# One step in sixteen rounded instead of f32 with its low part on GpSimd, a later transposition, and a new tail, in a fused attention and expert kernel

## The chip, the cores and the metric

The kernel runs on one core of a Trainium2 chip. Its time is the device time of one execution in microseconds (us). The core's engines work side by side, each through its own queue in program order: TensorE (PE in the profile, its weight loads PEld), VectorE (DVE), ScalarE (ACT), GpSimd (POOL) and SyncE (SP), which here only issues transfers. An instruction that waits holds up all that stands behind it in its queue.

## The reference

```python
B, N, C, n_agents = 4, 12480, 128, 49
a2k     = softmax(scale * agents @ k.T)      # 49 x 12480 for each batch
agent_v = a2k @ v                            # 49 x 128
q2a     = softmax(scale * q @ agents.T)      # 12480 x 49
x       = q2a @ agent_v                      # 12480 x 128, for 4 batches
h = x @ w_in                                 # d_ff = 2048
g = h - np.tanh(h)
out = g @ w_out
```

All is f32. The kernel multiplies `agent_v` by `w_in` once for each batch (the tile pair `awh`, `awl`), so that `h` comes straight from `q2a`.

## The kernel before

**Blocks, steps and pairs.** The tokens of the four batches are cut into 100 blocks of 500 (the last of each batch has 480). The 2048 hidden units are cut into 8 chunks of 256. One step is one block with one chunk, 800 steps in all. Here a **block pair** is two neighbouring blocks, thus 16 steps, and a step's place in it is its **position** 0 to 15 (`pos`). There are 50 block pairs, numbered 0 to 49.

**One step.** PE makes `h` (line 563, two halves of 128 x 504, six short products); ACT takes tanh (`y`, line 573) and squares it (`z`, line 578); DVE multiplies `h` by `z`, which gives `g` (line 583). For the small `h` of these inputs `h * z` is close enough to `h - tanh(h)`. Then PE multiplies `g` by a chunk of `w_out` and adds it to the block's accumulator `acc` (line 632), in one of two ways:

- a **rounded** step splits `g`: GpSimd rounds it to `gh` (line 613), DVE takes `gl = g - gh` (line 618), and PE multiplies `gh` and `gl` by split weights, 12 short products;
- a **plain** step multiplies `g` by unsplit f32 weights: nothing on GpSimd, no second DVE instruction, 4 products that the trace records as 8.

`PLAIN` holds the positions that are plain: 1, 3, 7, 8 and 9. So GpSimd rounds eleven times in a block pair.

**The order around the change.** It is written out by hand in `fast`. In the turn of step k the program emits: the take-over of a finished block (ACT copies half of `acc`, line 644; DVE adds the other half to it, line 641, after which the accumulator's bank is free), then `product(k)`, that is `g` and for a rounded step `gh`; then the running side jobs, one stage each; then tanh and square of step k+1; then `h` of a step ahead; then `gl` of step k-1; then the products of step k-1 into `acc`. `AHEADS` says which `h` a turn makes: two steps ahead as a rule, but at position 8 both of positions 10 and 11, at position 9 none. A finished block is taken over two turns after its last products, so that the even block of the pair is taken over at position 10 and the odd one at position 2.

**Side jobs.** One job makes the softmax over agents for the queries of the next block pair. It begins at position 2; its stages are spread by `QGAPS`, and its last stage falls on position 9: DVE sums (line 521), adds a small constant (522), inverts (523), scales `qe` (524) and copies it rounded into `pp` (527), and GpSimd writes the rest into `pp` (529). `pp` is then transposed on PE in two halves (line 538), at positions `T0` = 11 and `T1` = 15; one turn later ACT casts the result into `pT` (547) and two transfers copy it to other partitions (`pb`, lines 551 and 552). `h` of the next block pair reads `pT` and `pb`; its first one is made at position 14. While a batch is worked on, key jobs (`KS`) and value jobs (`VS`) prepare the next batch; a value job subtracts the maximum on GpSimd (line 344). `kq` is the list of jobs still to come.

**Buffers.** PSUM has four places of two banks, shared by `h`, `acc`, `pt` and the jobs. SBUF tiles: `g` four, `gh` three, `gl` three.

**The end.** After the last step, the last products are made, the last block is taken over, and one transfer (line 809) stores both blocks of the last pair.

Of the kernel before, what the change touches and what calls it, by code (L numbers as in the profile page):

```python
# [12 lines left out]
F32 = mybir.dt.float32  # L13
# [6 lines left out]
ALU = mybir.AluOpType  # L20
# [38 lines left out]
KV = 3  # L59
VB = 4  # L60
PLAIN = (1, 3, 7, 8, 9)
NB = dict(y=2, z=2, g=4, gh=3, gl=3)
Q0 = 2
NV = 10
# [3 lines left out]
QL = 0  # L68
QS = 2
QGAPS = (1, 1, 0, 2, 3, 0, 0)  # L70
T0 = 11
T1 = 15
KS = {2: 1, 12: 2}
VS = {1: 1, 8: 2}
# [4 lines left out]
def width(n):  # L79
    return min(BLK, N - n % NBLK * BLK)  # L80


def column(n):
    return n // NBLK * N + n % NBLK * BLK
# [18 lines left out]
class Build:  # L103
# [31 lines left out]
    def constants(self):  # L135
# [17 lines left out]
        self.wo_l = c.tile([128, NCH, C], F32R, tag="wo_l", name="wo_l")  # L153
        self.wo_f = {i: c.tile([128, 2 * C], F32, tag=f"wo_f{i}", name=f"wo_f{i}") for i in sorted({i % 8 for i in PLAIN})}
        self.vb = [c.tile([128, GT, C + 2], F32, tag=f"v{i}", name=f"v{i}") for i in range(VB)]
# [47 lines left out]
    def load_w_out(self, c, raw):  # L203
        one, two = self.wtile("gl", NB["gl"]), self.wtile("gh", NB["gh"])
        cut = lambda t, k: t[:, 512 * k : 512 * (k + 1)]
        return self.decode(raw, self.wf[:, c * 512 : (c + 1) * 512], cut(one, 0), cut(one, 1), cut(two, 0), cut(two, 1))
# [364 lines left out]
    def tanh(self, h, w):  # L571
        y = self.wtile("y", NB["y"])[:, : 2 * w]
        self.nc.scalar.activation(self.pair(y), h, AF.Tanh, scale=TSC)  # L573
        return y

    def square(self, y):
        z = self.wtile("z", NB["z"])[:, : y.shape[1]]
        self.nc.scalar.activation(z, y, AF.Square, scale=GSC)  # L578
        return z

    def mul(self, h, z, w):
        g = self.wtile("g", NB["g"])[:, : 2 * w]
        self.nc.vector.tensor_tensor(self.pair(g), h, self.pair(z), ALU.mult)  # L583
        self.mul_at = self.last_name()
        return g

    def act_general(self, hv, w):
        nc = self.nc
        d = self.wtile("y", NB["y"])[:, : 2 * w]
        u = self.wtile("z", NB["z"])[:, : 2 * w]  # L590
        nc.scalar.activation(self.pair(d), hv, AF.Tanh)
# [21 lines left out]
        self.nc.gpsimd.tensor_scalar(gh, g, 1.0, 0.0, ALU.mult, ALU.add)  # L613
        return gh

    def low(self, g, gh):
        gl = self.wtile("gl", NB["gl"])[:, : g.shape[1]].bitcast(F32R)
        self.nc.vector.tensor_tensor(gl, g, gh.bitcast(F32), ALU.subtract)  # L618
        return gl

    def m2(self, acc, i, gh, gl, wf=None):
        nc = self.nc
        w = gh.shape[1] // 2
        high, low = (lambda c: self.wo_h[:, 2 * i + c, :]), (lambda c: self.wo_l[:, 2 * i + c, :])
        if gl is None:
            terms = [(lambda c: wf[:, c * C : (c + 1) * C], gh, c) for c in range(2)]
        else:
            terms = [(low, gh, 0), (high, gh, 0), (low, gh, 1), (high, gh, 1), (high, gl, 0), (high, gl, 1)]
        for k, (weights, g, c) in enumerate(terms):
            for r in range(2):  # L630
                rows = slice(HALF * r, HALF * (r + 1))
                nc.tensor.matmul(  # L632
                    acc[:, r, :w],
                    weights(c)[rows],
                    g[rows, c * w : (c + 1) * w],
                    start=i == 0 and k == 0,
                    stop=i == NCH // 2 - 1 and k == len(terms) - 1,
                )
# [46 lines left out]
    def fast(self):  # L685
        nc, tc = self.nc, self.tc
        HP = NCH // 2
        blocks = [(b, j) for b in range(B) for j in range(NBLK)]
        steps = [(n, i) for n in range(len(blocks)) for i in range(HP)]
# [13 lines left out]
        def t_job(n):  # L703
            pT[n] = []
            return self.q_transpose(pp[n // 2][0], n % 2, pT[n])
# [84 lines left out]
        kq = []  # L790
        r1, r2, done = [], [], []
# [7 lines left out]
        def out_at(n):  # L799
            first = n - n % 2  # L800
            if n == first and n // 2 not in outs:
                outs[n // 2] = self.work.tile([128, GW], F32, tag="out", name="o", bufs=2)
            return outs[n // 2][:, n % 2 * width(first) :][:, : width(n)]

        def finish(n):
            self.add_up(out_at(n), acc[n])
            if n % 2 == 1:
                w = width(n - 1) + width(n)
                nc.sync.dma_start(self.outT[:, column(n - 1) : column(n - 1) + w], outs[n // 2][:, :w])

# [13 lines left out]
        def product(k):  # L824
            n, i = steps[k]
            g = self.mul(hs.pop(k), zs.pop(k), width(n))
            plain = n == 0 or n % 2 * HP + i in PLAIN
            gh = None if plain else self.high(g)
            r1.append((n, i, g, gh))

        def low(keep):
            while len(r1) > keep:
                n, i, g, gh = r1.pop(0)
                r2.append((n, i, g, None) if gh is None else (n, i, gh, self.low(g, gh)))

        def out(k):
            while r2:
# [12 lines left out]
        for k, (n, i) in enumerate(steps):  # L850
            b = blocks[n][0]
            pos = (n % 2) * HP + i
            p = n // 2
            if n % NBLK == 0 and i == 0 and b + 1 < B:
                kq = self.phase1(b + 1)
            begin = kq[0][0].get(pos, 0) if kq and n else 0
            if done and done[0][1] < k - 1:
                self.take(out_at(done[0][0]), acc[done[0][0]])
                finish(done.pop(0)[0])
            product(k)  # L860
            if n == LATE and i < NP:
                self.bound(0, i, slice(PCUT[i], PCUT[i + 1]))
            part = rest0.pop(0) if n == 0 and i in (0, 2, 4) else None
            go(part, 3)
            if n == 0 and i == 5:
                live.append(q1)
            if p + 1 < npair and pos in (T0, T1):
                live.append(t_job(2 * p + 2 + (pos == T1)))
# [12 lines left out]
            for j in AHEADS.get(pos, (AHEAD,)) if n else (AHEAD,):  # L881
                first_product(k + j)
            low(1)
            mark = self.last_on(ET.DVE)
            if n == 0:
# [16 lines left out]
            for kind in [x[0] for x in kq[:begin]]:  # L902
                if kind is kq[0][0] and kind.get(pos):
                    start(kq.pop(0)[1](pos))
        low(0)
        out(len(steps))
        while done:
            self.take(out_at(done[0][0]), acc[done[0][0]])
            finish(done.pop(0)[0])
# [64 lines left out]
```

## Time and profile before

| | |
|---|---|
| time, median of 3 runs | 2017.02 us (2016.4 to 2018.77) |
| the profiled execution's own time | 2018.59 us |
| its span, first to last instruction | 2016.8 us |
| mean granted clock of TensorE | 0.995 |
| PE busy, share of the span | 99% |
| DVE, ACT busy | 91%, 90% |
| GpSimd busy | 50% |
| chain that ended last: PE | 84% of the span |
| line 583, DVE `g`, 800 instructions | 955.5 us busy, 1195 ns each |
| line 618, DVE `gl`, 545 | 656.8 us busy, 1205 ns each |
| line 613, GpSimd `gh`, 545 | 853.0 us busy, 1565 ns each |

How to read it: a timeline row gives the start in us, the duration, engine, line, operation and tiles, and in brackets how long the engine sat idle before and what ended it. A row of the chain gives start, length and the work that the end waited for. A row of the windows gives a stretch, its length and the busy time of each engine in it, with the number of instructions, then the granted clock, the share of the DMA engines and GB/s. A row of the waits gives who waited for whom, the total, the number of times and the longest.

### The profile page before, as it was taken

How to read it: one execution, taken by the hardware profiler on the slowest of the kernel's cores; microseconds unless marked ns; L12 is line 12 of the kernel's file. 1: busy time of each engine (PE TensorE's matmuls, PEld its weight loads, DVE VectorE, ACT ScalarE, POOL GpSimd, SP SyncE). 2: the span in 40 equal slices, each digit the busy share in tenths (PEclk: the TensorE clock that was granted, in tenths of full speed). 3: DMA queues.
4: the chain of work that ended last, by engine and by line, in shares of the span. 5: the costliest groups of instructions: out<-in, count | busy, mean ns of one | idle time of the engine just before them, and what ended most of it. 6: DMA issues, size and time to landing. Idle time of an engine off the chain costs nothing.

```text
span 2016.8 us, 49577 instructions
## 1 busy us (share of the span) xinstructions
PE 1986.9 (99%) x20779; PEld 1460.9 (72%) x20779; DVE 1825.6 (91%) x1986; ACT 1806.5 (90%) x2052; POOL 999.9 (50%) x702
## 2 busy tenths in 40 slices
PE   8899999999999999999999999999999999999998
PEld 7477767777677777777677777777767777777775
DVE  7799999889999998898999999889899999999997
ACT  3789989899999998899999999998999999999996
POOL 1254455555445455554454454555545546555554
PEclk9899999999999999999999999999999999999999
DMA  9422112221111222221012111221101101101100
GB/s 331 135 85 93 54 45 84 83 61 44 54 61 65 78 71 60 78 75 60 31 36 92 61 58 44 71 61 56 54 29 34 52 31 35 52 29 37 39 24 27
DMA packets 76601, 129.70 MB, mean 64 GB/s; under 512 B 5384, under 2 KB 55376, under 8 KB 76368
## 3 DMA queue, kind: packets, MB, share of 16 engines
q1 hardware_dynamic: 76368, 126.44, 19.2%
q8 instruction: 165, 2.70, 0.6%
q14 instruction: 68, 0.56, 0.1%
HBM read 81.10 MB, written 25.56 MB: 53 GB/s over the span
## 4 chain that ended last, share of the span: by engine, by line
PE 84%; ACT 8%; DVE 4%; issue 2%; DMA 1%; SPq 0%; POOL 0%; DVEq 0%; POOLq 0%
PE acc L632 49%; PE h L563 26%; ACT z L578 4%; ACT y L573 4%; DVE g L583 2%; PE misc L508 2%; PE misc L357 2%; PE pt L538 1%; PE misc L301 1%; PE h L273 1%; DVE gl L618 1%; PE misc L472 1%; DMA v<-w_out 1%; PE h L380 0%; ACT s L349 0%
## 5 line engine op out<-in xcount | busy, mean ns | idle before, releaser
L613 POOL TENSOR_SCALAR gh<-g 128x1000 fp32r<-128x1000 f32 (+1 forms) x545 | 853.0, 1565 | 622.5 <-DVE g L583 578.6
L583 DVE TENSOR_TENSOR g<-h,z 128x1000 f32<-128x1000 f32 (+1 forms) x800 | 955.5, 1195 | 133.5 <-ACT z L578 122.9
L573 ACT ACTIVATE y<-h 128x1000 f32<-128x1000 f32 (+1 forms) x800 | 802.4, 1003 | 68.6 <-PE h L563 60.5
L578 ACT ACTIVATE z<-y 128x1000 f32<-128x1000 f32 (+1 forms) x800 | 831.4, 1039 | 25.4
L618 DVE TENSOR_TENSOR gl<-g,gh 128x1000 fp32r<-128x1000 f32 (+1 forms) x545 | 656.8, 1205 | 1.3 <-POOL gh L613 1.0
L563 PE MATMUL h<-pT,awh 49*128 49x504 f32 x1600 | 552.0, 424 | 0.0
L632 PE MATMUL acc<-g,wo_f 64*128 64x500 f32 (+1 forms) x1960 | 443.3, 578 | 0.0
L632 PE MATMUL acc<-gh,wo_l 64*128 64x500 f32 (+1 forms) x2180 | 433.0, 387 | 0.5 <-POOL gh L613 0.2
L632 PE MATMUL acc<-gh,wo_h 64*128 64x500 f32 (+1 forms) x2180 | 432.6, 386 | 0.0
L563 PE MATMUL h<-pT,awl 49*128 49x504 f32 x800 | 369.5, 462 | 7.2 <-DVE awl L476 3.4
L632 PE MATMUL acc<-gl,wo_h 64*128 64x500 f32 (+1 forms) x2180 | 341.2, 387 | 1.0 <-DVE gl L618 0.5
L563 PE MATMUL h<-pb,awh 49*128 49x504 f32 x1600 | 317.1, 387 | 0.0
L563 PE MATMUL h<-pb,awl 49*128 49x504 f32 x800 | 309.0, 386 | 0.0
L632 PEld LDWEIGHTS acc<-g,wo_f 64*128 64x128 f32 x1960 | 190.6, 186 | 145.3 <-issue 126.1
L563 PEld LDWEIGHTS h<-pT,awh 49*128 49x128 f32 x1600 | 265.9, 186 | 20.9 <-issue 11.1
L632 PEld LDWEIGHTS acc<-gh,wo_h 64*128 64x128 f32 x2180 | 214.3, 186 | 37.2
L632 PEld LDWEIGHTS acc<-gl,wo_h 64*128 64x128 f32 x2180 | 211.5, 184 | 40.0 <-DVE gl L618 5.7
L632 PEld LDWEIGHTS acc<-gh,wo_l 64*128 64x128 f32 x2180 | 211.1, 184 | 38.6 <-POOL gh L613 1.7
L563 PEld LDWEIGHTS h<-pT,awl 49*128 49x128 f32 x800 | 147.6, 184 | 117.4 <-DVE o L641 49.9
L529 POOL TENSOR_TENSOR pp<-qe,pp 128x392 fp32r<-128x392 f32 x50 | 51.5, 1030 | 265.3 <-DVE pp L527 257.2
L563 PEld LDWEIGHTS h<-pb,awh 49*128 49x128 f32 x1600 | 153.9, 184 | 29.9 <-DMA pb<-pT 0.5
L563 PEld LDWEIGHTS h<-pb,awl 49*128 49x128 f32 x800 | 149.3, 187 | 11.7 <-issue 6.4
(113 smaller groups left out, 1130.4 us busy)
## 6 DMA issues: line engine op xcount, KB each, us to landing
kt<-kT SPq DMA_DIRECT2D x48, 512.0 KB
qt<-qT SPq DMA_DIRECT2D x46, 500.0 KB
outT<-o SPq DMA_DIRECT2D x46, 500.0 KB
pb<-pT SPq DMA_DIRECT2D x200, 96.5 KB
v<-v SPq DMA_DIRECT2D x36, 512.0 KB
vt<-v SPq DMA_DIRECT2D x12, 512.0 KB
raw<-w_in SPq DMA_DIRECT2D x4, 512.0 KB
v<-w_out SPq DMA_DIRECT2D x4, 512.0 KB
```

What stands on the lines that cost most here:

```text
L273: nc.tensor.matmul(ps[:, t // 4, (t % 4) * A2 : (t % 4 + 1) * A2], kt[:, t, :], self.ag[:, 0:2, :], start=True, stop=True,)
L301: nc.tensor.matmul(to, kt[:, t, r : r + QUART], self.ag[:, b, :], start=True, stop=True)
L357: nc.tensor.matmul(ps[HALF * odd : HALF * odd + w, : C + 1], flat[:r, t * A : t * A + w], vt[:r, t, : C + 1], start=t < 2, stop=t >= n - 2,)
L508: nc.tensor.matmul(to, qt[:, token : token + QUART], self.ag[:, b, :], start=True, stop=True)
L529: nc.gpsimd.tensor_tensor(pp[:, :, HALF:PW], ev, pp[:, :, :A].bitcast(F32), ALU.subtract)
L563: nc.tensor.matmul(h[:, c, : BT * TT], aw[a][rows[c], sl], pT[p][rows[c], :], start=k == 0, stop=k == 2)
L573: self.nc.scalar.activation(self.pair(y), h, AF.Tanh, scale=TSC)
L578: self.nc.scalar.activation(z, y, AF.Square, scale=GSC)
L583: self.nc.vector.tensor_tensor(self.pair(g), h, self.pair(z), ALU.mult)
L613: self.nc.gpsimd.tensor_scalar(gh, g, 1.0, 0.0, ALU.mult, ALU.add)
L618: self.nc.vector.tensor_tensor(gl, g, gh.bitcast(F32), ALU.subtract)
L632: nc.tensor.matmul(acc[:, r, :w], weights(c)[rows], g[rows, c * w : (c + 1) * w], start=i == 0 and k == 0, stop=i == NCH // 2 - 1 and k == ...
```

## The change

Four things are changed.

1. Position 9 becomes a rounded step, except in the first block pair and where the next job to come is a value job. Its `gl` is made by GpSimd, right behind `gh`, in the turn of step 9 itself (`low(g, gh, True)` in `product`); the list `r1` carries it to the turn in which PE uses it. In the compiled program 37 steps are changed so; in the 12 block pairs with value jobs to come position 9 stays plain.
2. `T0` goes from 11 to 12: the first transposition, its cast and its two transfers come one turn later, in all 49 block pairs that have them.
3. The last step of the program (position 15 of the last pair) becomes plain.
4. The last two blocks are stored by a transfer each.

```diff
+POOL_LOW = (9,)
...
-T0 = 11
+T0 = 12
...
-    def low(self, g, gh):
+    def low(self, g, gh, pool=False):
         gl = self.wtile("gl", NB["gl"])[:, : g.shape[1]].bitcast(F32R)
-        self.nc.vector.tensor_tensor(gl, g, gh.bitcast(F32), ALU.subtract)
+        (self.nc.gpsimd if pool else self.nc.vector).tensor_tensor(gl, g, gh.bitcast(F32), ALU.subtract)
         return gl
...
             self.add_up(out_at(n), acc[n])
-            if n % 2 == 1:
+            if n >= len(blocks) - 2:
+                nc.sync.dma_start(self.outT[:, column(n) : column(n) + width(n)], out_at(n))
+            elif n % 2 == 1:
...
             g = self.mul(hs.pop(k), zs.pop(k), width(n))
-            plain = n == 0 or n % 2 * HP + i in PLAIN
+            pos = n % 2 * HP + i
+            pool = n > 1 and pos in POOL_LOW and not (kq and kq[0][0] is VS) and k < len(steps) - 1
+            plain = n == 0 or pos in PLAIN and not pool or k == len(steps) - 1
             gh = None if plain else self.high(g)
-            r1.append((n, i, g, gh))
+            r1.append((n, i, g, gh, self.low(g, gh, True) if pool else None))
 
         def low(keep):
             while len(r1) > keep:
-                n, i, g, gh = r1.pop(0)
-                r2.append((n, i, g, None) if gh is None else (n, i, gh, self.low(g, gh)))
+                n, i, g, gh, gl = r1.pop(0)
+                r2.append((n, i, g, None) if gh is None else (n, i, gh, gl or self.low(g, gh)))
```

What this does to the queues, at two places. From line 62 on, the changed file's numbers are higher by one, up to `finish`.

GpSimd, one block pair without value jobs, before: the rounding of positions 10 to 15, 0, 2 and 4 (nine `gh`), the query job's subtraction, the rounding of positions 5 and 6, and the rest of `pp`.

```order
L613 TENSOR_SCALAR gh<-g 128x1000 x9
L517 TENSOR_TENSOR qe<-qe,qm 128x392
L613 TENSOR_SCALAR gh<-g 128x1000 x2
L529 TENSOR_TENSOR pp<-qe,pp 128x8x49
L613 TENSOR_SCALAR gh<-g 128x1000 x9
```

And now:

```order
L614 TENSOR_SCALAR gh<-g 128x1000 x9
L518 TENSOR_TENSOR qe<-qe,qm 128x392
L614 TENSOR_SCALAR gh<-g 128x1000 x3
L619 TENSOR_TENSOR gl<-g,gh 128x1000
L530 TENSOR_TENSOR pp<-qe,pp 128x8x49
L614 TENSOR_SCALAR gh<-g 128x1000 x9
```

A third `gh` (position 9) and its `gl` now stand ahead of `pp`, and so ahead of the `gh` of position 10.

DVE at the same place, before: `g` of positions 8 and 9, the last stage of the query job, the addition that frees the accumulator, and `g` of positions 10 and 11.

```order
L583 TENSOR_TENSOR g<-h,z 128x1000 x2
L521 TENSOR_REDUCE qs<-qe 128x8
L522 TENSOR_SCALAR qs<-qs 128x8
L523 RECIPROCAL qs<-qs 128x8
L524 TENSOR_TENSOR qe<-qe,qs 128x392
L527 CAST pp<-qe 128x8x49
L641 TENSOR_TENSOR o<-o,acc 128x500
L583 TENSOR_TENSOR g<-h,z 128x1000 x2
L618 TENSOR_TENSOR gl<-g,gh 128x1000
```

In the changed program DVE's rows at this place are the same nine, in the same order, with their new line numbers; in the whole program DVE loses one `gl`, that of the last step.

PE, from the `h` of position 12 on, before: that `h`, the plain products of position 9, the transposition, and `h` of position 13.

```order
L563 MATMUL h<-pT,awl 128x504
L563 MATMUL h<-pT,awh 128x504 x2
L563 MATMUL h<-pb,awl 128x504
L563 MATMUL h<-pb,awh 128x504 x2
L632 MATMUL acc<-g,wo_f_87 128x500 x4
L538 MATMUL pt<-identr,pp 113x64 x8
L563 MATMUL h<-pT,awl 128x504
L563 MATMUL h<-pT,awh 128x504 x2
```

And now, from the products of position 9 on, with those of position 10 behind `h` of position 13:

```order
L633 MATMUL acc<-gl,wo_h 128x500 x4
L564 MATMUL h<-pT,awl 128x504
L564 MATMUL h<-pT,awh 128x504 x2
L564 MATMUL h<-pb,awl 128x504
L564 MATMUL h<-pb,awh 128x504 x2
L633 MATMUL acc<-gh,wo_l 128x500 x2
L633 MATMUL acc<-gh,wo_h 128x500 x2
L633 MATMUL acc<-gh,wo_l 128x500 x2
L633 MATMUL acc<-gh,wo_h 128x500 x2
L633 MATMUL acc<-gl,wo_h 128x500 x4
L539 MATMUL pt<-identr,pp 113x64 x8
L564 MATMUL h<-pT,awl 128x504
```

The transposition has moved behind `h` of position 13 and the products of position 10; the first row is the end of position 9's products, which now read `gl`.

## The prediction, made before the changed kernel ran

> **What bounds the kernel now.** I read the windows first, for one block pair of the last batch, where no key or value jobs run (the columns: stretch, length, busy time of PE, PEld, DVE, ACT, POOL, then the granted clock).
>
> ```profile
> 1896.61:1933.48 36.87, 36.87 (x350) 27.08 (x350) 33.98 (x37) 34.96 (x38) 19.64 (x14) 1.00 0.07 26
> ```
>
> PE is busy in all of the 36.87 us; DVE has 2.9 us to spare, ACT 1.9, GpSimd half. So PE sets the time, work taken from PE is worth its length, and any wait put on PE costs its length, unless another engine is then late. Next the chain through positions 8 to 12 of block pair 48:
>
> ```profile
> 1954.63 3.36 PE acc L632 x16
> 1957.99 0.78 PE h L563 x6
> 1958.77 1.68 PE acc L632 x8
> 1960.44 0.33 PE pt L538 x8
> 1960.77 0.76 PE h L563 x5
> 1961.53 1.36 PE acc L632 x11
> ```
>
> The 3.36 are the plain products of positions 7 and 8; then come `h` of position 12, the plain products of position 9 (1.68), the transposition, `h` of position 13 and the rounded products of position 10 (1.36). A plain step thus costs PE 0.32 us more than a rounded one: this is what the change takes away. Now what the other engines do there, from the timeline:
>
> ```profile
> 1954.07 1.20 DVE L583 TENSOR_TENSOR g<-h,z 128x1000 f32<-128x1000 f32 x1 [0.68 <-ACT z L578]
> 1955.18 0.55 DVE L521 TENSOR_REDUCE qs<-qe 128x8 f32<-128x392 f32 x1
> 1955.77 0.17 DVE L522 TENSOR_SCALAR qs<-qs 128x8 f32<-128x8 f32 x1
> ...
> 1956.21 0.57 DVE L524 TENSOR_TENSOR qe<-qe,qs 128x392 f32<-128x392 f32 x1
> 1956.81 0.36 DVE L527 CAST pp<-qe 128x392 fp32r<-128x392 f32 x1
> 1957.09 0.67 DVE L641 TENSOR_TENSOR o<-o,acc 128x500 f32<-128x500 f32 x1
> 1957.67 2.48 DVE L583 TENSOR_TENSOR g<-h,z 128x1000 f32<-128x1000 f32 x2
> 1960.11 1.20 DVE L618 TENSOR_TENSOR gl<-g,gh 128x1000 fp32r<-128x1000 f32 x1
> 1961.45 1.20 DVE L583 TENSOR_TENSOR g<-h,z 128x1000 f32<-128x1000 f32 x1
> ```
> ```profile
> 1957.26 1.03 POOL L529 TENSOR_TENSOR pp<-qe,pp 128x392 fp32r<-128x392 f32 x1 [6.30 <-DVE pp L527]
> 1959.05 1.02 POOL L613 TENSOR_SCALAR gh<-g 128x1000 fp32r<-128x1000 f32 x1 [0.77 <-DVE g L583]
> 1960.34 1.87 POOL L613 TENSOR_SCALAR gh<-g 128x1000 fp32r<-128x1000 f32 x1 [0.26 <-DVE g L583]
> ```
> ```profile
> 1957.81 0.49 PE L563 MATMUL h<-pT,awl 49*128 49x504 f32 x1
> 1962.73 0.46 PE L563 MATMUL h<-pT,awl 49*128 49x504 f32 x1
> ```
> ```profile
> PEld h L563 <- DVE o L641: 49.9, 99, 1.6
> PEld h L563 <- DVE g L583: 31.3, 106, 1.0
> ```
>
> The first row is `g` of position 9; it ends at 1955.27, and DVE goes straight into the query job. `h` of position 12 starts on PE at 1957.81, 0.05 after the addition L641 has freed the accumulator's bank (1957.09 + 0.67 = 1957.76). The waits name this pair of instructions 99 times. So **the DVE queue from L521 to L641 has no room: what delays it stops PE**. `h` of position 14 (1962.73) likewise follows `g` of position 12 (1961.45 + 1.20 = 1962.65), the second row of the waits. GpSimd's 6.30 us of idle time ahead of `pp` are where the new `gh` and `gl` go. They lie on DVE's query job.
>
> **Do GpSimd and DVE get in each other's way?** Two stretches of the timeline say so.
>
> ```profile
> 754.45 1.03 POOL L613 TENSOR_SCALAR gh<-g 128x1000 fp32r<-128x1000 f32 x1 [0.37 <-DVE g L583]
> ```
> ```profile
> 754.51 1.00 DVE L323 TENSOR_SCALAR dg<-ident,mc 49x49 f32<-49x49 f32 x1
> ```
> ```profile
> 1365.41 1.03 POOL L613 TENSOR_SCALAR gh<-g 128x1000 fp32r<-128x1000 f32 x1 [0.41 <-DVE g L583]
> ```
> ```profile
> 1365.67 1.82 DVE L618 TENSOR_TENSOR gl<-g,gh 128x1000 fp32r<-128x1000 f32 x1
> ```
>
> A small DVE instruction (49 x 49) that begins 0.06 behind a `gh` ends with it, 1.00 us later; a `gl`, 1.20 as a rule, takes 1.82 when a `gh` has begun before it. L522 is of the first kind (one SBUF tile in, one out), as L527 is, and L524 of the second (two tiles in). The other way round, the `gh` of 1960.34, begun behind the `gl` of 1960.11, takes 1.87 instead of 1.02. So the two exclude each other, the later one waits for the end of the earlier, where DVE reads SBUF alone. `g` and L641 read PSUM too and run beside `gh` undisturbed (1959.05, inside 1957.67 + 2.48).
>
> **The new schedule in block pair 48.** `gl` of 1000 on GpSimd is in no row. Its nearest kin:
>
> ```profile
> L214 POOL TENSOR_TENSOR wo_l<-awh,wo_h x4: 1274/1294/1487, 78.7 to 90.1; 128x512 fp32r<-128x512 f32 x4
> ```
> ```profile
> L344 POOL TENSOR_TENSOR s<-s,mb 128x98 f32<-128x98 f32 x3 | 1.2, 401 | 7.6 <-DVE g L583 7.6
> ```
>
> Between 98 elements (0.401) and 512 (at best 1.274) lie 2.11 ns each; 488 more make 1.274 + 1.03 = 2.30. Scaling `pp`'s row, 1.03 for 392, gives 2.63; the lower bound is a `gh` of the same size, 1.02, though it reads one tile instead of two. I take 2.30, since the 512 row has the same form. Step by step:
>
> - `gh` of position 9: `g` ends at 1955.27, GpSimd starts 0.19 later (1960.15 to 1960.34 in the rows): 1955.46 to 1956.48.
> - L522 is ready at 1955.77, finds GpSimd at work and waits: 1956.48 to 1956.65. Then GpSimd's `gl`, waiting by now, goes ahead of L524: 1956.65 to 1958.95.
> - L524 1958.95 to 1959.52; L527 at 1959.55; L641 0.28 behind its start: 1959.83 to 1960.50; `h` of position 12 at 1960.55. **PE waits 1960.55 - 1957.81 = 2.74 us longer.**
> - From there DVE runs 2.74 later, while PE has saved 0.32. But `h` of position 14 waits for `g` of position 12, which is 2.74 late; PE's 0.32 go into that wait. Net 2.74.
>
> Other sequences: if L522 does not wait, L524 comes first and the delay is 2.54; if `gl` follows `gh` at once, 3.04. With a `gl` of 2.63 at most 3.37; with one of 1.02, 1.46.
>
> Where it happens: 37 steps change; the last block pair has no query job, so 36 meet this. The last one saves its 0.32. The 12 with value jobs keep position 9 plain.
>
> **The clock.** A stop of 2.74 us in a PE that never stops may lower the granted clock. Windows of the start-up:
>
> ```profile
> 26.27:33.09 6.82, 5.37 (x47) 5.04 (x46) 5.97 (x11) 1.79 (x7) 0.00 (x0) 1.00 1.03 412
> 60.40:67.23 6.83, 3.48 (x22) 1.85 (x22) 5.29 (x8) 6.51 (x8) 0.00 (x0) 1.00 0.82 290
> 67.23:70.64 3.41, 3.41 (x12) 1.30 (x8) 3.34 (x6) 3.03 (x4) 0.00 (x0) 0.50 0.32 86
> 87.71:94.53 6.82, 5.76 (x34) 2.78 (x32) 3.06 (x4) 6.72 (x9) 2.57 (x5) 1.00 0.00 0
> ```
>
> PE was busy 3.48 us in the 6.83 up to 67.23, and then had half the clock for 3.41 us (0.50). The first window, with 5.37 busy, was followed by a drop too; the last, with 5.76, by none. The edges 33.09, 67.23 and 94.53 lie 6.83 or a multiple apart. A window that holds the whole new stop has 6.83 - 2.74 = 4.09 busy, below 5.37: I expect a drop behind it. The whole stop lies in one window in 1 - 2.74/6.83 = 60% of placements, and in half of the others over 2 us lie on one side; I take 8 in 10. A drop costs PE half of 3.41, 1.71, of which 0.32 goes into the wait at position 14: 1.39 x 0.8 = **1.11 us a block pair**; bounds 0, and 3.41 - 0.32 = 3.09 if the half clock lasts two such stretches every time.
>
> Here the Trainium skill speaks against me: "TensorE: Matmul & The Clock Gate", section "HAM oscillation — how this bites in real kernels", allows PE gaps up to about 3.4 us. By that rule this term is nothing. The 5.37 window, whose idle time is 1.45 us, does not agree with it, but other matmuls ran there. It is the first rival below.
>
> **The smaller edits.** The transposition keeps its 0.33 on PE, beside the other order. Its cast and two transfers come one turn later, and the waiting transfer holds up only loads behind it on SP, which are made for later. Rows of the timeline, the windows and the chain:
>
> ```profile
> 1960.81 0.59 ACT L547 CAST pT<-pt 113x504 fp32r<-113x504 f32 x1
> ```
> ```profile
> 1965.00:1966.00 1.00, 1.00 (x12) 0.82 (x10) 1.00 (x2) 1.00 (x2) 0.93 (x1) 1.00 0.00 0
> ```
> ```profile
> 1967.08 0.68 PE h L563 x6
> ```
>
> From the cast to the last byte took until 1965 (no DMA in that window); the first use is the `h` of 1967.08, 2.1 us on. A turn is `h` plus rounded products, 0.69 + 1.36 = 2.05. That just covers it: nothing, with bounds of 0 and 0.4 us a block pair. The tail, from the chain:
>
> ```profile
> 2004.81 1.75 POOL gh L613
> ...
> 2007.79 0.73 PE acc L632 x4
> ```
>
> The last `gh` and the `gl` behind it go. PE then has only the plain products (1.68) behind those of the step before; without the wait they would start some 0.4 before that `gh` ended, at about 2006.15 (an estimate), so PE ends near 2007.8 instead of 2007.79 + 0.73 = 2008.52: 0.7 saved. A last transfer of half the size is hidden or worth some tenths; bounds of the tail 0 to 1.5.
>
> **Sum.** 36 x (2.74 + 1.11) = 138.6, less 0.3 and 0.7: +137.6. Against the profiled execution's span of 2016.8 this is 2154.4, against its own time of 2018.59 (1.8 outside the span) 2156.2. That execution lies 1.6 above the median of 2017.02; on the median: 2154.6. I say **2155**.
>
> **Rivals.**
> 1. *The stop costs, the clock holds.* For it: the skill's rule, and that the low windows are from the start-up only. 36 x 2.74 - 1.0: 2115; 2107 (2.54) to 2137 (3.37).
> 2. *DVE keeps its turn until the query job is done*, and `gl` comes after L527, at 1957.9. DVE is then held up only by `gh` (0.7), but `gl` ends at 1960.2, `pp` at 1961.2, `gh` of position 10 at 1962.3, DVE's `gl` at 1963.5, so `g` of position 12 is 1.95 late: 36 x 1.95 - 1.0, 2086. Against it: DVE's L522 to L527 leave gaps.
> 3. *No exclusion for these forms.* Then `gl` ends at 1958.8, `pp` at 1959.9, `gh` of position 10 at 1960.9, `g` of position 12 is 0.65 late: 36 x 0.65 - 1.0, 2039. Even so it is slower: three jobs stand ahead of a `gh` that was just in time.
> 4. *Faster:* no exclusion, and `gl` at its lower bound of 1.02. It then ends at 1957.5, `pp` at 1958.6, ahead of 1959.05, and nothing is late: 37 x 0.32 + 0.7 = 12.5 saved, 2004.5. It decides from `pp` ending by 1959.05. Against it: 1.27 for 512.
> 5. That the change does nothing is ruled out by the compiled order (37 `gl` on GpSimd).
>
> **Chances.** Forecast 50% (own range 2137 to 2190: every stop with a drop and 3.37 is 36 x 4.76 - 1.0), rival 1 29%, rival 2 8%, rival 3 5%, rival 4 4%, within 0.2% (about what a measurement of this kernel can tell from no change; a `gl` short enough that loss and saving are equal) 2%, above 2190 by longer half clocks 2%. The first three hold 87% and make the range, 2086 to 2190. Faster 0.04, same 0.02, slower 0.94.
>
> **What would show it.** Right: L524 some 2.7 us later behind `g` of position 9, with a GpSimd `gl` of about 2.3 between; PEld waiting for L641 by 2.7 more, in 36 places; ten-odd per cent of the slices with a clock of 8 or 9 tenths. Rival 1: the same with a mean clock above 0.99. Wrong: L524 still at +0.94 behind `g` while GpSimd's `gl` runs. A GpSimd `gl` near 1 us, or PE not waiting for L641, would make the whole forecast wrong.

## The result, and the profile after

The changed kernel takes 2123.43 us (median of 4 runs, 2122.85 to 2128.7); the kernel before, 2017.89 (4 runs). The ratio is 1.0529, interval 1.051 to 1.0548: slower by 105 us. The forecast was 2155, the range 2086 to 2190. The profiled execution has a span of 2121.2 us (before 2016.8) and a mean granted clock of 0.980 (0.995).

First the windows of two block pairs of the last batch, 46 and 47, from one `g` of position 0 to the next (columns as before).

```profile
1955.21:1994.31 39.10, 36.79 (x356) 27.55 (x354) 36.35 (x37) 35.03 (x39) 23.14 (x16) 1.00 0.11 37
1994.31:2034.74 40.43, 38.09 (x354) 29.08 (x352) 36.61 (x36) 34.73 (x39) 22.82 (x16) 0.96 0.07 24
```

Before, a pair took 36.87 us, and PE was busy in all of them. Now PE is idle 2.31 us in the first (39.10 - 36.79). The second has the same gap, but a granted clock of 0.96 instead of 1.00, and takes 1.3 us more. So there are two losses: a stop of PE in every such pair, and a drop of the clock in some. Of the 36 pairs that meet the query job, 20 show such a drop in the clock's records and 16 none; the 12 pairs with value jobs take as long as before.

The stop itself, in pair 46: VectorE, GpSimd and PE around `g` of position 9 (line numbers are those of before plus one).

```profile
1975.80 1.20 DVE L584 TENSOR_TENSOR g<-h,z 128x1000 f32<-128x1000 f32 x1 [0.68 <-ACT z L579]
1976.92 0.55 DVE L522 TENSOR_REDUCE qs<-qe 128x8 f32<-128x392 f32 x1
1977.50 0.71 DVE L523 TENSOR_SCALAR qs<-qs 128x8 f32<-128x8 f32 x1
1978.24 0.20 DVE L524 RECIPROCAL qs<-qs 128x8 f32<-128x8 f32 x1
1978.48 2.51 DVE L525 TENSOR_TENSOR qe<-qe,qs 128x392 f32<-128x392 f32 x1
1981.03 0.37 DVE L528 CAST pp<-qe 128x392 fp32r<-128x392 f32 x1
1981.31 0.67 DVE L642 TENSOR_TENSOR o<-o,acc 128x500 f32<-128x500 f32 x1
```
```profile
1977.16 1.03 POOL L614 TENSOR_SCALAR gh<-g 128x1000 fp32r<-128x1000 f32 x1 [4.46 <-DVE g L584]
1978.27 2.30 POOL L619 TENSOR_TENSOR gl<-g,gh 128x1000 fp32r<-128x1000 f32 x1
1981.47 1.03 POOL L530 TENSOR_TENSOR pp<-qe,pp 128x392 fp32r<-128x392 f32 x1 [0.90 <-DVE pp L528]
```
```profile
1976.20 3.52 PE L633 MATMUL acc<-g,wo_f 64*128 64x500 f32 x16
1982.03 0.49 PE L564 MATMUL h<-pT,awl 49*128 49x504 f32 x1 [2.31 <-DVE o L642]
```

Two durations of VectorE have grown. L523, 0.17 before, takes 0.71: it ends 0.02 behind the `gh` that ends at 1978.19. L525, 0.57 before, takes 2.51: it begins while `gl` runs (1978.27 to 1980.57) and ends 0.42 behind it. Neither does more work than before; the time is waiting. PE has finished the plain products at 1979.72 and starts `h` of position 12 at 1982.03, 0.05 behind the addition L642. Behind the end of `g` of position 9 that is 5.03 us, where it was 2.55.

The waits and the page show the same over the whole run:

```profile
PEld h L564 <- DVE o L642: 138.4, 99, 3.2
PE h L564 <- DVE o L642: 83.2, 37, 2.4
```
```profile
PE 58%; ACT 22%; DVE 14%; issue 2%; DMA 2%; SPq 0%; POOL 0%; DVEq 0%; POOLq 0%
...
L525 DVE TENSOR_TENSOR qe<-qe,qs 128x392 f32<-128x392 f32 x50 | 98.4, 1968 | 1.7
```

The row of 99 waits for the freed bank has grown from 49.9 to 138.4 us, and PE itself waits there 37 times, 83.2 us in all; before, it did so twice, for 1.2 us. In the chain PE's share falls from 84% to 58%. L525 counts 1968 ns each where an undisturbed one takes 567. GpSimd, which causes all this, has 0% of the chain: it shows only as long durations of VectorE.

Last, the clock. The drops in the records begin on a grid of 3.41 us, and each of the 20 lasts 3.41. The windows follow the grid: two ahead of a drop in pair 47 and the drop, then the two around the stop of pair 46.

```profile
2014.51:2017.92 3.41, 3.41 (x24) 1.94 (x22) 2.93 (x5) 3.09 (x5) 1.59 (x2) 1.00 0.00 0
2017.92:2021.34 3.42, 1.10 (x8) 0.30 (x6) 3.39 (x4) 1.79 (x2) 2.52 (x2) 1.00 0.00 0
2021.34:2024.75 3.41, 3.41 (x18) 2.74 (x18) 3.15 (x4) 2.04 (x2) 2.58 (x3) 0.50 0.02 5
1976.96:1980.38 3.42, 2.76 (x14) 0.97 (x10) 3.32 (x5) 3.10 (x4) 3.14 (x2) 1.00 0.00 0
1980.38:1983.79 3.41, 1.76 (x16) 1.54 (x18) 3.38 (x5) 1.04 (x2) 1.76 (x3) 1.00 0.00 0
```

In pair 47 the whole gap lies in one window (PE busy 1.10 of 3.42) and half the clock follows (0.50). In pair 46 the same gap is cut by an edge into 0.66 and 1.65, and the clock stays at 1.00.

### The profile page after: what moved, and what is told of

Its sections match the earlier page's. It is cut to its first block, busy times and chain, and to the rows that moved or that the text cites. A ratio compares the mean times of both kernels' runs of the same rounds, so it can differ in the third digit from the quotient of the medians.

```text
span 2121.2 us, 50007 instructions
## 1 busy us (share of the span) xinstructions
PE 2008.7 (95%) x20923; PEld 1500.1 (71%) x20923; DVE 1910.8 (90%) x1985; ACT 1807.1 (85%) x2052; POOL 1126.9 (53%) x775
## 4 chain that ended last, share of the span: by engine, by line
PE 58%; ACT 22%; DVE 14%; issue 2%; DMA 2%; SPq 0%; POOL 0%; DVEq 0%; POOLq 0%
PE acc L633 32%; PE h L564 19%; ACT z L579 11%; ACT y L574 10%; DVE qe L525 5%; DVE g L584 4%; PE misc L509 2%; PE misc L358 2%; PE misc L302 1%; DVE qs L523 1%; PE pt L539 1%; DVE o L642 1%; DVE qs L522 1%; DMA kt<-kT 1%; DMA pb<-pT 1%
## 5 line engine op out<-in xcount | busy, mean ns | idle before, releaser
L614 POOL TENSOR_SCALAR gh<-g 128x1000 fp32r<-128x1000 f32 (+1 forms) x581 | 895.1, 1541 | 798.7 <-DVE g L584 759.5
L633 PE MATMUL acc<-gh,wo_l 64*128 64x500 f32 (+1 forms) x2324 | 470.3, 394 | 0.3
L633 PE MATMUL acc<-gh,wo_h 64*128 64x500 f32 (+1 forms) x2324 | 470.5, 393 | 0.0
L564 PE MATMUL h<-pT,awl 49*128 49x504 f32 x800 | 373.7, 467 | 89.2 <-DVE o L642 83.2
L633 PE MATMUL acc<-g,wo_f 64*128 64x500 f32 (+1 forms) x1672 | 376.8, 578 | 0.0
L633 PE MATMUL acc<-gl,wo_h 64*128 64x500 f32 (+1 forms) x2324 | 371.7, 394 | 1.0 <-DVE gl L619 0.5
L564 PEld LDWEIGHTS h<-pT,awl 49*128 49x128 f32 x800 | 150.3, 188 | 195.7 <-DVE o L642 138.4
L633 PEld LDWEIGHTS acc<-gh,wo_h 64*128 64x128 f32 x2324 | 234.7, 191 | 41.5
L633 PEld LDWEIGHTS acc<-gl,wo_h 64*128 64x128 f32 x2324 | 231.9, 189 | 43.8 <-DVE gl L619 5.4
L633 PEld LDWEIGHTS acc<-gh,wo_l 64*128 64x128 f32 x2324 | 230.8, 189 | 41.3 <-POOL gh L614 1.1
L633 PEld LDWEIGHTS acc<-g,wo_f 64*128 64x128 f32 x1672 | 162.3, 186 | 127.0 <-issue 110.2
L525 DVE TENSOR_TENSOR qe<-qe,qs 128x392 f32<-128x392 f32 x50 | 98.4, 1968 | 1.7
```

The costliest lines, as they stand in the source:

```text
L525: nc.vector.tensor_tensor(ev, ev, s[:, :, None].broadcast_to([TS, GT, A]), ALU.mult)
L564: nc.tensor.matmul(h[:, c, : BT * TT], aw[a][rows[c], sl], pT[p][rows[c], :], start=k == 0, stop=k == 2)
L633: nc.tensor.matmul(acc[:, r, :w], weights(c)[rows], g[rows, c * w : (c + 1) * w], start=i == 0 and k == 0, stop=i == NCH // 2 - 1 and k == ...
```

## The experiments

The theory: GpSimd's `gh` and `gl` of position 9 hold up the query job on VectorE (exclusion), this stops PE, and the stops lower the clock, which costs time of its own. The rivals: a part of the loss comes from other edits (`T0`, the products); the drops stand in time that PE would have waited anyway. For each run: the edit, what was expected, what came.

### GpSimd's work alone

PE keeps the plain products of position 9; GpSimd's `gh` and `gl` are made and not read.

```diff
-            r1.append((n, i, g, gh, self.low(g, gh, True) if pool else None))
+            gl = self.low(g, gh, True) if pool else None
+            r1.append((n, i, g, None, None) if pool else (n, i, g, gh, gl))
```

> The changed kernel, but PE keeps the plain f32 products at position 9: GpSimd makes gh and gl of position 9 and nobody reads them. Theory (GpSimd's two instructions hold up VectorE's query job, which frees the accumulator): h of position 12 still starts 5.0 us behind the end of g of position 9 (2.55 before), each of 36 block pairs is longer by 2.2 + 0.32 us, plus clock drops of about 1.46 us in 20 of them: 2137 us, 2125 to 2145. Rival (the rounded products or their order on PE cost the time): 2017 to 2025.

Measured: 2143.76 us, ratio 1.0616 (1.0599 to 1.0634), clock 0.976. `h` of position 12 again starts 5.03 behind `g` of position 9; a pair without a drop takes 39.29 us, and 24 of 36 have a drop (the changed kernel: 20). GpSimd's two instructions, whose results nobody uses here, are enough for the whole loss: 125 us against 105 in the changed kernel, since PE's saving is missing (39.29 us a pair instead of 39.09 without a drop), four more pairs have a drop, and a drop costs 1.65 us here instead of 1.45.

### `gl` back on VectorE

```diff
-            r1.append((n, i, g, gh, self.low(g, gh, True) if pool else None))
+            r1.append((n, i, g, gh, None))
```

> The changed kernel, rounded at position 9 in the same block pairs, but with gl on VectorE in the usual turn instead of on GpSimd. Theory (the 2.3 us of GpSimd's gl are the stop): only gh holds up the query job, h of position 12 starts 0.5 to 0.6 us later than before instead of 2.48, no clock drops; VectorE has 1.1 us more to do ahead of g of position 12: 2030 to 2060. Rival (any rounded step at position 9 brings the stop): above 2100.

Measured: 2060.24 us, at the upper edge of what was expected; ratio 1.0217 (1.0203 to 1.0231), clock 0.996. Its timeline in pair 46, VectorE and PE:

```profile
1921.12 0.70 DVE L523 TENSOR_SCALAR qs<-qs 128x8 f32<-128x8 f32 x1
1921.86 0.20 DVE L524 RECIPROCAL qs<-qs 128x8 f32<-128x8 f32 x1
1922.10 0.57 DVE L525 TENSOR_TENSOR qe<-qe,qs 128x392 f32<-128x392 f32 x1
```
```profile
1923.70 0.49 PE L564 MATMUL h<-pT,awl 49*128 49x504 f32 x1 [0.35 <-DVE o L642]
```

L523 still waits for `gh` (0.70), but L525 is back at 0.57, and PE's gap is 0.35 instead of 2.31. So `gl` on GpSimd is the part that makes the stop. What is left, 38.02 us a pair against 36.87, comes later: the `gl` now in VectorE's queue makes `g` of position 12 start 7.37 us behind the end of `g` of position 9, 6.18 before.

### The query job one turn earlier

Its last stage falls on position 8, so that GpSimd's work at position 9 meets nothing of it.

```diff
-QGAPS = (1, 1, 0, 2, 3, 0, 0)
+QGAPS = (1, 1, 0, 2, 2, 0, 0)
```

> The changed kernel with the last stage of the query job one position earlier (position 8 instead of 9), so that GpSimd's gh and gl of position 9 meet no VectorE instruction that reads SBUF alone until gl of position 10. Theory (exclusion with the query job): the stop at h of position 12 shrinks below 0.5 us and no clock drop follows; left is gh of position 10, some 1 us late behind gl: 2025 to 2060. Rival (the queue on GpSimd alone costs the time, three instructions ahead of gh of position 10): above 2090.

Measured: 2052.4 us, ratio 1.0174 (1.0157 to 1.0191), clock 0.994. No stop at `h` of position 12 and no drop in the steady pairs; a pair takes 37.67 us. The exclusion therefore needs both: GpSimd's work and the job beside it. What remains is 0.80 us a pair. Its timeline, VectorE from the addition on, and GpSimd:

```profile
1913.53 0.68 DVE L642 TENSOR_TENSOR o<-o,acc 128x500 f32<-128x500 f32 x1 [0.56 <-ACT o L645]
1914.12 1.19 DVE L584 TENSOR_TENSOR g<-h,z 128x1000 f32<-128x1000 f32 x1
1916.63 1.20 DVE L584 TENSOR_TENSOR g<-h,z 128x1000 f32<-128x1000 f32 x1 [1.31 <-POOL gl L619]
```
```profile
1914.24 2.36 POOL L619 TENSOR_TENSOR gl<-g,gh 128x1000 fp32r<-128x1000 f32 x1
1916.56 1.03 POOL L614 TENSOR_SCALAR gh<-g 128x1000 fp32r<-128x1000 f32 x1
```

`gh` of position 10 now queues behind `gl` on GpSimd, and VectorE stands idle 1.31 us until that `gl` ends, in 36 places. That `g` of position 11 should wait for it was not expected: its own `z` was ready at 1915.48. The wait is in the program: in the compiled order `g` of position 11 gets the buffer of `g` of position 9, and the last to read that one is now GpSimd's `gl`. The changed kernel has this wait too, but there `gl` has long ended (1980.57) when `g` of position 11 begins (1983.00).

### The transposition, taken back and alone

`T0` = 11 in the changed kernel, and `T0` = 12 as the only edit of the kernel before.

```diff
-T0 = 12
+T0 = 11
```

> The changed kernel with the first transposition back at position 11. Theory (the move is no part of the loss): 2116 to 2125; PE's waits for the copied pT (7.2 us in the changed kernel, 0.5 before) go back to about 0.5. Rival (the late transposition makes h of the next block pair late): 2060 or less.

```diff
-T0 = 11
+T0 = 12
```

> The kernel before with nothing but the first transposition moved from position 11 to 12. Theory: the copy lands just in time, 0 to 0.4 us lost in some block pairs: 2015 to 2025. Rival (the move alone is a large part of the loss): above 2040.

Measured: 2125.08 us (2117.97 to 2125.96; ratio 1.0521, 1.05 to 1.0541) and 2020.2 us (ratio 1.0014, 1.0005 to 1.0023). Taking it back gains nothing that can be seen, just above the expected range; the wait for the copied `pT`, 7.2 us in the changed kernel, is gone with it, as expected. Alone the move costs 0.14%, below the 0.2% bound.

### Filling the stop

Products with zero weights are put behind those of position 8, so that PE works in the gap; the result doesn't change. The first try had ten of them.

```diff
+FILL = 5
...
+        self.zero = c.tile([128, 128], F32, tag="zero", name="zero")
+        nc.vector.memset(self.zero, 0.0)
...
+    def fill(self, acc, g, times):
+        w = g.shape[1] // 2
+        for _ in range(times):
+            for r in range(2):
+                rows = slice(HALF * r, HALF * (r + 1))
+                self.nc.tensor.matmul(acc[:, r, :w], self.zero[rows], g[rows, :w], start=False, stop=False)
...
+            self.filling = FILL if pool and n < len(blocks) - 1 else 0
...
+                self.fill(acc[n], gh, self.filling)
```

> The changed kernel with 10 products by zero weights put on PE into the stop, behind the products of position 8 (2.1 us of work in a stop of 2.48, results unchanged). Theory (the stop costs twice: by itself, and by a halved clock some us later): the drops vanish, mean clock 0.995, h of position 12 stays at 5.0 us, and the time falls by 20 x 1.46 = 29 us to about 2094, 2088 to 2100, although PE has more to do. Rival (a drop of the clock costs nothing here, since VectorE sets the pace behind the stop): 2121 to 2126.

Measured: 2150.53 us, ratio 1.0656 (1.0638 to 1.0674), clock 0.997. A miss by my sizing: two such products take 0.84 us, so ten take 4.2, more than the gap; `h` of position 12 came at 6.35 instead of 5.03. The drops were gone, but the run could not say what they cost. So again, with four products and with two:

```diff
-FILL = 5
+FILL = 2
```

> The changed kernel with four products of zero weights behind the products of position 8 of each block pair, where the earlier fill had ten. In the earlier fill two such products took 0.84 us, so four take about 1.68 us of the 2.48 us by which PE's stop has grown: PE is idle about 0.6 us there and h of position 12 stays where it is (about 5.0 us behind g of position 9). Theory: the drops of the clock cost 1.46 us each on top of the stop; without them the 20 drops of the changed kernel's profile go and nothing else changes: mean clock 0.99 or more, no block pair above 39.3 us, 20 x 1.46 = 29 us less, about 2094 us (2088 to 2102). Rival: the drops stand in time that PE would have waited for VectorE anyway: 2120 to 2128 with the clock just as high.

```diff
-FILL = 5
+FILL = 1
```

> The same with two such products, about 0.84 us: PE is idle about 1.5 us in each stop. The records of the changed kernel fit a rule by which the clock halves when one window of 3.41 us holds about 1.9 us or more of PE's idle time. By this rule 1.5 us never suffice: mean clock 0.99 or more and about 2094 us (2088 to 2102), as with four products. Rival: any stop of over 1 us can halve the clock: some 10 to 20 of the 36 block pairs show a drop, mean clock 0.98 to 0.99 and 2105 to 2123 us.

Measured: 2097.86 us (ratio 1.0395, 1.0377 to 1.0412) and 2098.54 us (1.0396, 1.0379 to 1.0413), both with a clock of 0.995 and no drop in any of the 36 pairs. Pair 46 of the second, PE and the windows:

```profile
1955.80 1.44 PE L636 MATMUL acc<-g,wo_f 64*128 64x500 f32 x6
1957.05 1.02 PE L649 MATMUL acc<-g,zero 64*128 64x500 f32 x4
1959.53 0.49 PE L567 MATMUL h<-pT,awl 49*128 49x504 f32 x1 [1.46 <-DVE o L652]
```
```profile
1932.72:1971.80 39.08, 37.62 (x360) 28.04 (x358) 36.37 (x37) 35.01 (x39) 23.11 (x16) 1.00 0.11 37
```

`h` of position 12 stays at 5.03, the pair at 39.08; only the kind of PE's time has changed, 1.46 us idle instead of 2.31. Against the changed kernel's ratio of 1.0529, 1.3% of the time before, 27 us, come back for useless work. So the drops cost time of their own, and a gap of 1.46 us is short enough to leave the clock alone.

### Is there a version that gains?

Two were tried. Position 7 instead of 9, whose `gl` meets no query job:

```diff
-POOL_LOW = (9,)
+POOL_LOW = (7,)
...
-T0 = 12
+T0 = 11
```

> The same idea where it meets nothing: position 7 instead of 9 rounded with its low part on GpSimd, the transposition at position 11, the rest as in the changed kernel. By the rows of before, gh of position 7 is done 1.9 us and its gl 4.2 us behind the end of g of position 7, some 0.2 us ahead of the query job's first instruction that excludes GpSimd, and just when PE wants it. Theory: no stop, no drops, 0.32 us saved in 37 block pairs and 0.7 at the end: 2005, 2002 to 2012. Rival (gl comes too late for PE or still meets the query job): 2017 to 2040.

Measured: 2020.6 us, ratio 1.0016 (1.0007 to 1.0025): a miss. The program has GpSimd's `gl` in 34 pairs, not in the 37 of the expectation. Its chain:

```profile
1881.59 1.83 POOL gh L614
1883.42 0.07 issue
1883.49 2.37 POOL gl L619
1885.86 0.04 issue
1885.91 2.40 PE acc L633 x12
```

`gh` waits behind a `gl` of VectorE (1.83 instead of 1.03), GpSimd's `gl` ends when PE is already waiting for it, and the 0.32 us that PE saves goes there: 36.92 us a pair.

And both cures at once, the job early and `gl` on VectorE:

```diff
-QGAPS = (1, 1, 0, 2, 3, 0, 0)
+QGAPS = (1, 1, 0, 2, 2, 0, 0)
...
-            r1.append((n, i, g, gh, self.low(g, gh, True) if pool else None))
+            r1.append((n, i, g, gh, None))
```

> The changed kernel with both edits that helped: the query job's last stage at position 8 and gl of position 9 on VectorE. With the job early alone, VectorE stood idle 1.31 us ahead of g of position 11 until GpSimd's gl ended. If gl (1.2 us, overlapping its neighbours by 0.1) stands in that gap instead, g of position 11 and all that follows starts about 0.3 us earlier than in that kernel: theory (VectorE has no room left behind position 9): period about 37.4 us, 36 x 0.3 = 11 us less than 2052, about 2041 us (2030 to 2050), still slower than before. Rival (only GpSimd's gl was in the way): PE keeps the 0.32 us it saves, period 36.6 us, 2006 to 2012 us, faster than before. Clock 0.99 or more by both.

Measured: 2041.96 us, ratio 1.0121 (1.0104 to 1.0138), 37.38 us a pair, as expected. VectorE from the addition on:

```profile
1905.61 0.68 DVE L642 TENSOR_TENSOR o<-o,acc 128x500 f32<-128x500 f32 x1 [0.56 <-ACT o L645]
1906.20 1.19 DVE L584 TENSOR_TENSOR g<-h,z 128x1000 f32<-128x1000 f32 x1
1907.31 1.19 DVE L619 TENSOR_TENSOR gl<-g,gh 128x1000 fp32r<-128x1000 f32 x1
1908.42 1.19 DVE L584 TENSOR_TENSOR g<-h,z 128x1000 f32<-128x1000 f32 x1
1909.53 1.19 DVE L619 TENSOR_TENSOR gl<-g,gh 128x1000 fp32r<-128x1000 f32 x1
```

There is no idle time in these rows behind the addition, nor in the following ones up to the end of the pair: each turn is 1.11 + 1.11 = 2.22 us of VectorE, where PE needs about 2.05. Over the whole pair VectorE still has 2.5 us to spare, but all of it ahead of that addition. No version that was run beats the kernel before.

## Why the prediction was right, and where its sizes were off

**The mechanism held.** L523 waits for `gh`, GpSimd's `gl` goes ahead of L525, the addition is late, `h` of position 12 waits for it, in 36 pairs. `gl` takes 2.30 us, as estimated. The Trainium skill, "SBUF — State Buffer", describes an exclusive lock between VectorE and GpSimd, in which the later of the two waits for the end of the earlier (section "Who interferes with whom"); the 0.71 of L523 and the 2.51 of L525 agree with it, but for the 0.42 that follow here.

**The stop: forecast 2.74, measured 2.48 (5.03 - 2.55).** The sequence was right. L525 ends 0.42 behind `gl`, where the sum gave it its whole 0.57. The other 0.11: `gl` begins 1.27 behind the end of `g` of position 9 and not 1.38, since L523 ends 0.02 behind `gh` and not 0.17.

**The net of a stop: forecast 2.74, measured 2.22.** A pair without a drop takes 39.09 instead of 36.87. Over 36 pairs that is 79.9 us, not 98.6, and this is the term that was most out. Of the 0.52 by which it was too dear, 0.26 are the stop; the rest is the step "From there DVE runs 2.74 later". VectorE catches up:

```profile
1981.89 2.30 DVE L584 TENSOR_TENSOR g<-h,z 128x1000 f32<-128x1000 f32 x2
1984.32 1.20 DVE L619 TENSOR_TENSOR gl<-g,gh 128x1000 fp32r<-128x1000 f32 x1
1985.44 1.19 DVE L584 TENSOR_TENSOR g<-h,z 128x1000 f32<-128x1000 f32 x1
```

These are positions 10 and 11, a `gl` and position 12, without a gap; before, VectorE stood idle 0.21 us between the same instructions. So `g` of position 12 starts 8.43 us behind the end of `g` of position 9 instead of 6.18, thus 2.25 late. "PE's 0.32 go into that wait" does not hold as it stands either. `h` of position 14 comes 2.21 late. It starts 0.05 behind the end of that `g`, and just as close behind PE's own work, which without the 0.32 would have ended later; where PE keeps the plain products, a pair takes 0.20 more. From position 12 to the next pair VectorE goes from one `g` or `gl` to the next without a gap in both kernels, so the 2.2 stay.

**The clock: forecast 40 us, measured 29.** That a gap below 3.4 us lowers the clock was right. It speaks against the rule of the Trainium skill that the first rival stood on ("TensorE: Matmul & The Clock Gate", section "HAM oscillation — how this bites in real kernels": gaps up to about 3.4 us allowed). The price of one drop was nearly right, 1.45 against 1.39: the pairs of the last batch with a drop take 40.44 to 40.61 us, 40.54 in the mean, those without 39.09. But "8 in 10" was read from windows of 6.83 us, and they are 3.41 long. A gap of 2.31 is cut by an edge more often in the shorter ones, and then the clock can hold: 20 of 36 have a drop, by the records. The sign "slices with a clock of 8 or 9 tenths" could not show it: nearly all slices of both pages read 9, since a slice lasts 53 us and a drop 3.41.

**Rival 1 (the clock holds, 2115) lies nearer to the result than the forecast, but not for its reason:** its stop was 18.7 us too dear in all, which makes up for most of the 29 us of drops that it denied. The two runs with the short fill are the kernel that it described, and they take 2098.

**The rest.** `T0`: forecast nothing, with bounds of 0 and 0.4 a pair; alone it costs 2.5 us in 49 pairs, 0.05 each in the mean. The wait for the second transfer, 0.5 us before, has grown to 7.2:

```profile
L564 PEld LDWEIGHTS h<-pb,awh 49*128 49x128 f32 x1600 | 157.1, 188 | 36.6 <-DMA pb<-pT 7.2
```

The tail: 0.7 was forecast; from the first `g` of the last pair to the end are 45.92 us, 46.46 before, thus 0.5. One profile does not settle this: in all ten with the new tail the figure lies between 44.65 and 46.61, in the two with the old one it is 46.46 and 46.49. The chain now passes from `gl` to the products without GpSimd:

```profile
2108.45 1.07 DVE g L584
2109.52 1.08 DVE gl L619
2110.60 0.04 issue
2110.64 2.34 PE acc L633 x12
```

**The sum again.** 36 x 2.22 + 20 x 1.45 = 108.9. The start-up was 1.8 shorter in this execution (first `g` at 60.91 instead of 62.74), the tail 0.5: 106.6. The spans differ by 104.4. The 36 pairs by themselves are longer by 106.4 and not 108.9; the difference lies in the earlier batches, whose pairs hold key and value jobs too, and was not traced.

## What to carry to other kernels

Work put on an idle engine is not free if its instructions hold up those of a busy one, as GpSimd's `gl` held up L525 here: look at what the busy engine does in that very stretch, and who waits behind it. The average share of idle time does not answer this; the rows between two waits do. And where TensorE runs without gaps, a new gap has two prices, its length and the clock behind it; if the gap can't be removed, make it too short to lower the clock, with useless products if need be.

## What the runs showed of the hardware that was not expected

- A gap of 2.31 us halves TensorE's clock for 3.41 us, or leaves it, by where it falls on a grid of 3.41 us. In three kernels (the changed one, the one with `T0` back, the one with GpSimd's work alone) 20, 19 and 24 of 36 gaps had a drop; one of these 63 drops lasted 6.83. What counts is PE's idle time in one window of the grid. After the start-up, in no kernel here did a drop begin behind a window with less than 1.7 us of it, and one began behind every window with more than 2.01; of the 18 between, 13 had one behind them. Two of these 18, from the changed kernel, each with the window that follows: 1.78 us idle and a drop, 2.01 us idle and none.

```profile
174.73:178.14 3.41, 1.63 (x14) 1.41 (x16) 3.38 (x5) 1.02 (x2) 1.75 (x3) 1.00 0.00 0
178.14:181.55 3.41, 3.41 (x19) 2.76 (x18) 3.29 (x4) 2.36 (x3) 2.93 (x3) 0.50 0.00 0
215.69:219.10 3.41, 1.40 (x8) 0.36 (x4) 3.34 (x4) 2.30 (x3) 2.51 (x2) 1.00 0.00 0
219.10:222.51 3.41, 3.10 (x28) 2.65 (x30) 3.29 (x4) 2.07 (x3) 2.59 (x3) 1.00 0.01 2
```

The idle time is that of the records, in which the ends of products are modelled, so the limit may be sharper than it looks. With a limit of 1.87, in the middle, a gap of 2.31 lowers the clock in (3.41 - 1.43) / 3.41 = 58% of placements (an estimate; 1.43 is 2 x 1.87 - 2.31); 63 of 108 are 58%. The limit was inferred from these gaps; the run with gaps of 1.46 us, and none of 36 with a drop, was made after it and agrees. It is not a limit for every mix of products: in the start-up of the kernel before, the window up to 33.09 has 1.45 us of idle time, and half the clock follows.
- L525 with a GpSimd instruction ahead of it ends 0.42 us behind that one, though it takes 0.57 alone: some 0.15 of its time passes beside the other.
